# Scales of operands from norms summed by a matmul with ones, on one core, in place of maxima sent through small transfers

## The chip, the cores and the metric

The kernel runs on one core of one Trainium2 chip. A core has TensorE (PE; its weight loads are shown apart, as PEld), VectorE (DVE), ScalarE (ACT), GpSimd (POOL) and SyncE (SP, which here only issues transfers). Each of them works through its own instructions in the order in which they stand in the program, and waits on semaphores for the others. The metric is the device time of one execution in microseconds (us), the median of several.

## The reference

Three stages follow one another, in float32. The sizes are 2304 tokens and a width of 512.

```python
# 1. attention in chunks of 64 tokens, 8 heads of 64
scores = scale * np.matmul(q_c, k_c.transpose(0, 1, 2, 4, 3))
attn = np.exp(scores - np.max(scores, axis=-1, keepdims=True))
attn = attn / (np.sum(attn, axis=-1, keepdims=True) + 1e-09)
out = np.matmul(attn, v_c)
# 2. four experts, 512 -> 1024 -> 512
p = domain_probs / (domain_probs.sum(-1, keepdims=True) + 1e-09)
for e in range(E):
    out += p[:, e:e + 1] * (np.maximum(x @ w1[e], 0.0) @ w2[e])
# 3. a gated layer, 512 -> 1536 -> 512
g = x @ w_gate
return (g * (1.0 / (1.0 + np.exp(-g))) * (x @ w_val)) @ w_out
```

## The kernel before

Every matmul of stages 2 and 3 runs on float16 pairs: an operand is split into a high part (ACT) and a rest (mostly POOL, some DVE), and three float16 products replace one float32 product. float16 has little range, so each operand is first multiplied by a power of two that is worked out from its values: this is its **scale**, and how it is found is what the change is about.

Tokens go in three passes of 768, as six blocks of 128. Stage 2 has 16 **sets** of weights per pass (256 columns of `w1` each), stage 3 has 12. A set is seven half-size products in place of eight (Strassen's scheme, `PRODUCTS`), each 6 matmuls of 384 columns, into PSUM banks `x`, `z` and `w`; ACT copies intermediate sums (`p`, `u`) out of a bank before the next product adds to it, DVE adds them up (`sum_p`, `sum_u`), ACT and DVE make the float16 pair of the hidden layer (`hh`, `hl`). The second matmul of a layer (`y`, or `ox` and `oz`) is placed between the products. In pass 0 the weights come as float32 (`raw`), are scaled, summed, split and stored as float16 (`w`); passes 1 and 2 load the stored ones. The weights of stage 3 come as 64-bit floats and are converted by background tasks (`make_ops`) during passes 0 to 2.

The order is written by hand, as a program that is played out product by product. `now` counts products; `later(d, f)` calls `f` after product `now + d`. A background task advances once per product; `yield WAIT` in it is one product of delay. Attention of blocks 0 to 5 comes first, by a table of steps (`FIRST_BLOCKS`); blocks 6 to 17 (`rest`) are put in steps between the products of pass 0.

A scale before, for a set of `w1` that was loaded in pass 0: `greatest` (DVE) reduces 128x1024 values to one maximum per partition (`col`); `spread_out` writes this column to DRAM, `spread_in` reads it back as one row on all partitions (`row`), both on SP's queue; `spread_end` (DVE) reduces the row, `scale_of` makes the power of two, and ACT multiplies (`w1_scaled`). `w2` (`w2_scale_later`), the 64-bit sets (`spread`, `row`) and `wo` (`spread_wo`, `row_wo`) do the same. Only the first five scales go by `total`, a matmul of `ones` with a bfloat16 column, which leaves the sum over partitions on all of them. The attention output has a scale for each token (`att_scale`), from the maxima of the block's own `av` in PSUM.

Of the kernel before, what the change touches and what calls it, by code (L numbers as in the profile page):

```python
# [94 lines left out]
def attention_moe_gated(  # L95
# [26 lines left out]
    by_token = const.tile([P, NS], F32, name="by_token")  # L122
# [42 lines left out]
    def scale_of_norm(o, back, left, square, k):  # L165

        nc.vector.tensor_scalar_max(square, square, TINY)
        halve(o, square)
        flip(o, o)
        nc.vector.tensor_scalar(out=o, in0=o, scalar1=2.0 ** (k - 66), scalar2=None, op0=ALU.mult)  # L170
        flip(back, o)
        nc.vector.scalar_tensor_tensor(out=left, in0=square, scalar=o, in1=o, op0=ALU.mult, op1=ALU.mult)
# [16 lines left out]
    def total(col, name, where):  # L189
        pool, tag = where  # L190
        ps = pool.tile([P, 512], F32, tag=tag, name=f"total_{name}")[:, :1]
        nc.tensor.matmul(ps, ones, col, start=True, stop=True)
        return ps
# [200 lines left out]
    def att_sums(a):  # L394
        s = att[a]
        sm = st_p.tile([P, H], F32, tag="sm", name=f"sm{a}")
        part = s["hs"][:, :, :, : CH // 4] if a < HALF else pairs(s["e"])
        nc.vector.tensor_reduce(out=by_pair(sm), in_=part, op=ALU.add, axis=AX.X)
        nc.vector.tensor_scalar_add(sm, sm, EPS)
        s["rs"] = st_p.tile([P, H], F32, tag="rs", name=f"rs{a}")  # L400
        nc.vector.reciprocal(s["rs"], sm)

# [16 lines left out]
    def att_scale(a):  # L419
        s = att[a]  # L420
        ps = s.pop("av")
        tops = st_p.tile([P, H], F32, tag="tops", name=f"tops{a}")
        top = st_p.tile([P, 1], F32, tag="top", name=f"top{a}")
        own = by_token[:, a : a + 1]
# [8 lines left out]
        if a >= BLOCKS and a % BLOCKS == BLOCKS - 1:  # L433
            scaled_shares(a // BLOCKS)

    def scaled_shares(s):
        r = slice(s * BLOCKS, (s + 1) * BLOCKS)
        nc.vector.tensor_scalar(
            out=back[:, r].bitcast(I32), in0=by_token[:, r].bitcast(I32), scalar1=EXPONENT, scalar2=None, op0=ALU.bitwise_xor
        )  # L440
# [62 lines left out]
    def fetch_w1(n, own=True):  # L503
        r = raw1[n] = raw1_p.tile([P, 8, 2 * P], F32, tag="raw1", name=f"raw1_{n}")
        nc.sync.dma_start(r[:, 0:4], w1[weights_of(n)])
        if n >= NPAIRS:
            later(3, lambda: w1_scaled(n))
        elif own:
            col = small(f"col_{n}")
# [4 lines left out]
            def ended():  # L514
                o = small(f"sum_{n}")
                spread_end(f"w1_{n}", o, ALU.add)
                w1_scale_of(n, o)
                w1_scaled(n)

            later(8, ended)  # L520

    def w1_scale_of(n, bound):
        s, r = w1_scale[n], w1_back[n] = small(f"s1_{n}"), small(f"b1_{n}")
        scale_of(s, bound, 9)
        flip(r, s)
# [69 lines left out]
    def make_ops(sources, name, sums, stores, column, scaled):  # L595
# [16 lines left out]
        col = small(f"col_{name}")  # L612
        op = column(r, col)
        yield WAIT
        spread_out(name, col)
        yield WAIT
        yield WAIT
        spread_in(name)
        yield WAIT
        yield WAIT  # L620
        bound = small(f"bound_{name}")
        spread_end(name, bound, op)
        scale = small(f"scale_{name}")
        scaled(scale, bound)
# [10 lines left out]
    def make_set64(q, m):  # L635
        into = w_d[NPAIRS + 2 * q + m]
        stores = [(PRODUCTS[i][1], into[i]) for i in range(NPROD)]

        def column(r, col):
            rows = small(f"rows_{q}_{m}", 4)  # L640
            for half in range(2):
                nc.vector.tensor_reduce(
                    out=rows[:, 2 * half : 2 * half + 2],
                    in_=r[:, 2 * half : 2 * half + 2].rearrange("p b (k f) -> p k b f", k=2),
                    op=ALU.max, axis=AX.XY, apply_absolute_value=True,
                )
            nc.vector.tensor_tensor(out=rows, in0=rows, in1=rows, op=ALU.mult)
            nc.vector.tensor_reduce(out=col, in_=rows, op=ALU.add, axis=AX.X)
            return ALU.add

        def scaled(scale, bound):
            scale_of_norm(scale, again64[:, m, q : q + 1], left64[:, m, q : q + 1], bound, 12)

        return make_ops(
            (wg, wv)[m][q], f"{q}_{m}", lambda r, half: w_sums(r, nc.gpsimd, half), stores, column, scaled
        )

    def make_wo_ops(g, k):
# [10 lines left out]
        def column(r, col):  # L669
            greatest(col, r[:, 0:4].rearrange("p b f -> p (b f)"))  # L670
            return ALU.max

        def scaled(scale, bound):
            scale_of(scale, bound, 10)
            flip(again64[:, 2, 2 * g + k : 2 * g + k + 1], scale)
# [8 lines left out]
    def x1_norm(s, b, sum_):  # L684
        a = s * BLOCKS + b
        waste = t_p.tile([P, DM], F16, tag="waste", name=f"waste_{a}", bufs=1)
        nc.scalar.activation(waste, sum_, AF.Square, accum_out=norms[:, a : a + 1])

    def x1_bound(s):
# [5 lines left out]
        later(3, lambda: spread_in(f"x1_{s}"))  # L695

        def ended():
            spread_end(f"x1_{s}", bound, ALU.max)
            x1_left[p] = small(f"x1_left_{s}")
            scale_of_norm(x1_scale[p], x1_back[p], x1_left[p], bound, 10)  # L700
# [3 lines left out]
        later(5, ended)  # L704
# [70 lines left out]
    def w2_greatest(G, i):  # L775
        c = w2_cols[G, i] = small(f"col2_{G}_{i}")
        greatest(c, raw2[G, i].rearrange("p b f -> p (b f)"))

    def w2_col(G, dtype=F32):
        c0, c1 = w2_cols[G, 0], w2_cols[G, 1]  # L780
        o = small(f"cols2_{G}", 1, dtype)
        nc.vector.tensor_scalar(out=c1, in0=c1, scalar1=w1_back[2 * G + 1], scalar2=None, op0=ALU.mult)
        nc.vector.scalar_tensor_tensor(out=o, in0=c0, scalar=w1_back[2 * G], in1=c1, op0=ALU.mult, op1=ALU.max)
        return o

    def w2_scale_of(G, bound):
        s = small(f"s2_{G}")
        w2_back[G] = small(f"b2_{G}")
        scale_of(s, bound, 11)
# [9 lines left out]
    def w2_scale_later(G, d):  # L799
# [4 lines left out]
        def out():  # L804
            spread_out(f"w2_{G}", w2_col(G))

        def ended():
            o = small(f"sum2_{G}")
            spread_end(f"w2_{G}", o, ALU.add)
            w2_scale_of(G, o)  # L810
            w2_scaled(G, 0)
# [235 lines left out]
    def gather(G, b, y):  # L1047
# [5 lines left out]
        if part == 1:  # L1053
            if b == 0:
                pg[0] = sm_p.tile([P, BLOCKS], F32, tag="pg", name=f"pg_{G}")
                nc.vector.tensor_scalar(
                    out=pg[0], in0=shares_of[:, s * BLOCKS : (s + 1) * BLOCKS, g * NE // NG1], scalar1=w2_back[g], scalar2=0.125,
# [28 lines left out]
    with tc.manual_schedule():  # L1086
# [5 lines left out]
        sm_p = ctx.enter_context(tc.tile_pool(name="sm", bufs=3))  # L1092
        w_p = ctx.enter_context(tc.tile_pool(name="w", bufs=12))
# [86 lines left out]
        def own_col(n):  # L1180
            cols[n] = small(f"col_{n}", 1, BF16)
            greatest(cols[n], raw1[n][:, 0:4].rearrange("p b f -> p (b f)"))
# [18 lines left out]
        def at(stage):  # L1201
# [6 lines left out]
            "f": lambda n: fetch_w1(n, False), "F": fetch_w1, "k": att_load_v, "L": att_load,  # L1208
            "a": own_col, "b": own_scale, "A": lambda i: w2_greatest(0, i), "B": lambda i: own_col2(), "C": lambda place: own_scale2(place),
# [34 lines left out]
        for a in range(BLOCKS, NS + 2):  # L1244
            for stages in ((att_scores, a), (att_values, a - 2)), (), ((att_turn, a - 1),), ((att_out, a - 2),):
                these = [(stage, b) for stage, b in stages if BLOCKS <= b < NS]
# [3 lines left out]
        def next_of_rest():  # L1250
            for stage, a in rest.pop(0):
                stage(a, (psA, "a"))
# [60 lines left out]
        for j in range(4):  # L1313
            later(6 + j, lambda j=j: split_w2(1, j))
# [25 lines left out]
        for o in order:  # L1340
# [29 lines left out]
            if i == 0 and (n == FIRST or group_of(n) != group_of(n - 1)) and group_of(n) < NPASS * NG1:  # L1370
# [5 lines left out]
                elif n > FIRST:  # L1376
                    w2_scale_later(G, 4)
                    for j in range(4):
                        later(1 + j // 2, lambda G=G, j=j: fetch_w2(G, j))
                        later(10 + j, lambda G=G, j=j: split_w2(G, j))  # L1380
# [104 lines left out]
```

## Time and profile before

| what | value |
|---|---|
| median of 3 runs (lowest to highest) | 1409.56 us (1405.64 to 1409.64) |
| the profiled execution | 1412.3 us, of which 1410.2 us from the first to the last instruction |
| PE busy | 1206.8 us (86%) |
| DVE, ACT, POOL busy | 927.5 us (66%), 609.7 us (43%), 536.2 us (38%) |
| mean granted TensorE clock | 0.938 |

PE has the most work. Its idle time and its clock are what another order of the work can change; busy time of another engine counts only where PE comes to wait for it.

### The profile page before, as it was taken

The numbers are of one execution on the slowest core, as the hardware profiler recorded it, in microseconds if no ns is written. First come the engines' busy times: TensorE is split into PE (matmuls) and PEld (weight loads), VectorE is DVE, ScalarE is ACT, GpSimd is POOL, SyncE is SP. The second block draws the span as 40 slices with busy tenths as digits, with TensorE's granted clock in tenths as the row PEclk, the third lists the DMA queues.
The fourth block names the chain that finished last, engine by engine and source line by source line (L and its number), as shares of the span: only waits on it lengthen the run. The fifth ranks groups of instructions, "written<-read, shape, count | busy, mean of one in ns | idle before, by whom it ended". The sixth has DMA issues, their size and how long they took to land.

```text
span 1410.2 us, 21408 instructions
## 1 busy us (share of the span) xinstructions
PE 1206.8 (86%) x7221; PEld 703.4 (50%) x7221; DVE 927.5 (66%) x1852; ACT 609.7 (43%) x1285; POOL 536.2 (38%) x603
## 2 busy tenths in 40 slices
PE   6888858857476998887889987979999999999998
PEld 5554435423233554443445443435556667676666
DVE  7787566655575576556755565643766786687677
ACT  4534433433345544344445443432454354444442
POOL 5233222323466555555553465551013322222221
PEclk9998979878698999999999999999999999999999
DMA  7277637538565676756576577765447655454543
GB/s 219 82 130 203 143 125 170 106 129 225 96 161 155 188 190 197 188 131 192 148 232 170 138 171 198 199 155 178 127 127 196 202 181 180 137 186 149 185 130 109
DMA packets 191085, 230.08 MB, mean 163 GB/s; under 512 B 25584, under 2 KB 146544, under 8 KB 190976
## 3 DMA queue, kind: packets, MB, share of 16 engines
q1 hardware_dynamic: 190048, 227.25, 59.5%
q10 hardware_dynamic: 896, 1.44, 0.3%
q8 instruction: 56, 0.92, 0.3%
q14 instruction: 53, 0.43, 0.1%
q0 software_dynamic: 32, 0.04, 0.0%
HBM read 168.60 MB, written 60.05 MB: 162 GB/s over the span
## 4 chain that ended last, share of the span: by engine, by line
PE 39%; DMA 26%; DVE 17%; issue 7%; ACT 7%; POOL 3%; SPq 1%; DVEq 0%; POOLq 0%; ACTq 0%
PE lx L917 4%; PE lx L918 4%; PE lx L919 4%; PE oz L1035 4%; DMA row_w<-spread_w 3%; DMA spread_w<-col 3%; PE ox L1035 3%; DMA w<-w 3%; PE y L966 3%; PE y L970 3%; PE y L968 3%; DMA spread_wo<-col_wo 2%; PE lz L917 2%; DVE col L145 2%; PE lz L918 2%
## 5 line engine op out<-in xcount | busy, mean ns | idle before, releaser
L966 PE MATMUL y<-w,hh 128*128 128x512 f16 x576 | 224.9, 390 | 7.3 <-ACT hh L847 3.9
L970 PE MATMUL y<-w,hl 128*128 128x512 f16 x576 | 223.4, 388 | 7.8 <-DVE hl L848 7.8
L135 POOL TENSOR_TENSOR w<-raw,w 128x256 f16<-128x256 f32 (+1 forms) x156 | 127.2, 827 | 258.3 <-ACT w L134 205.7
L968 PE MATMUL y<-w,hh 128*128 128x512 f16 x576 | 223.6, 388 | 0.0
L918 PEld LDWEIGHTS <-w 128*128 128x128 f16 x1182 | 118.6, 100 | 167.4 <-issue 96.9
L135 POOL TENSOR_TENSOR ol<-sg,oh 128x384 f16<-128x384 f32 x72 | 75.3, 1054 | 316.5 <-ACT oh L134 260.2
L917 PEld LDWEIGHTS <-w 128*128 128x128 f16 x1182 | 118.4, 100 | 120.0 <-DMA w<-w 36.2
L919 PEld LDWEIGHTS <-w 128*128 128x128 f16 x1182 | 119.1, 101 | 83.8 <-issue 11.0
L847 ACT ACTIVATE hh<-sum_p 128x384 f16<-128x384 f32 x90 | 46.8, 520 | 156.8 <-DVE sum_p L905 156.8
L848 DVE SCALAR_TENSOR_TENSOR hl<-sum_p,hh 128x384 f16<-128x384 f32 x90 | 60.2, 669 | 72.8 <-ACT hh L847 72.8
L1064 DVE SCALAR_TENSOR_TENSOR acc<-y,pg,acc 128x512 f32<-128x512 f32 x126 | 90.6, 742 | 25.5 <-PE y L970 23.1
L970 PEld LDWEIGHTS <-hl 128*128 128x128 f16 x576 | 57.6, 100 | 82.5 <-DVE hl L848 11.5
L966 PEld LDWEIGHTS <-hh 128*128 128x128 f16 x576 | 57.8, 100 | 71.6 <-issue 8.0
L135 POOL TENSOR_TENSOR w_made<-raw,w_made 128x256 f16<-128x256 f32 x84 | 61.3, 738 | 81.3 <-ACT w_made L134 73.8
L968 PEld LDWEIGHTS <-hh 128*128 128x128 f16 x576 | 57.7, 100 | 66.9 <-issue 9.0
L917 PE MATMUL lz<-b22h,w 128*128 128x384 f16 x162 | 54.6, 337 | 33.7 <-ACT p L901 33.3
L917 PE MATMUL lx<-t2h,w 128*128 128x384 f16 x162 | 54.6, 337 | 32.4 <-ACT p L901 32.2
L905 DVE TENSOR_TENSOR sum_p<-lx,p 128x384 f32<-128x384 f32 x81 | 44.6, 551 | 42.2 <-PE lx L919 41.4
L134 ACT ACTIVATE w<-raw 128x256 f16<-128x256 f32 (+1 forms) x156 | 67.6, 450 | 0.7 <-DVE raw L539 0.3
L917 PE MATMUL lz<-t1h,w 128*128 128x384 f16 x162 | 56.5, 349 | 12.8 <-DMA w<-w 12.6
L917 PE MATMUL lx<-t3h,w 128*128 128x384 f16 x162 | 53.3, 329 | 13.2 <-ACT u L901 8.4
L917 PE MATMUL lx<-b11h,w 128*128 128x384 f16 x162 | 55.2, 341 | 9.3 <-DMA w<-w 9.3
(282 smaller groups left out, 3012.3 us busy)
## 6 DMA issues: line engine op xcount, KB each, us to landing
w<-w SPq DMA_DIRECT2D x567, 128.0 KB, 3.6
w<-w SPq DMA_DIRECT2D x96, 256.0 KB, 4.9
w<-w_made SPq DMA_DIRECT2D x84, 128.0 KB, 4.7
raw<-w SPq DMA_DIRECT2D x19, 512.0 KB, 5.2
wo_t<-wo_t SPq DMA_DIRECT2D x36, 256.0 KB, 3.3
raw<-w SPq DMA_DIRECT2D x32, 256.0 KB, 4.8
sums<-x SPq DMA_DIRECT2D x40, 192.0 KB, 4.6
xt<-sums SPq DMA_DIRECT2D x40, 192.0 KB, 3.4
```

Source lines behind the costliest of these rows:

```text
L134: nc.scalar.activation(h, src, AF.Copy)
L135: (lo or nc.vector).tensor_tensor(out=l, in0=src, in1=h, op=ALU.subtract)
L847: nc.scalar.activation(h, src, AF.Relu)
L848: nc.vector.scalar_tensor_tensor(out=l, in0=src, scalar=0.0, in1=h, op0=ALU.max, op1=ALU.subtract)
L917: nc.tensor.matmul(ps, w[:, 0, c], xh[:, k], start=f, stop=False, skip_group_check=True)
L918: nc.tensor.matmul(ps, w[:, 0, c], xl[:, k], start=False, stop=False, skip_group_check=True)
L919: nc.tensor.matmul(ps, w[:, 1, c], xh[:, k], start=False, stop=e, skip_group_check=True)
L966: nc.tensor.matmul(y, hh[:, c], w[:, 0], start=(j == 0), stop=False)
L968: nc.tensor.matmul(y, hh[:, c], w[:, 1], start=False, stop=False)
L970: nc.tensor.matmul(y, hl[:, c], w[:, 0], start=False, stop=(j == 3))
L1035: nc.tensor.matmul(o, left[:, c], w[:, k, right], start=start and t % 2 == 0 and k == 0 and i == 0, stop=k == 1 and i == 2, skip_group_che ...
L1064: nc.vector.scalar_tensor_tensor(out=sum_, in0=y, scalar=p, in1=sum_, op0=ALU.mult, op1=ALU.add)
```

## The change

Maxima become sums of squares. `squares` is one ACT instruction over 128x1024 values that writes its squares to a scratch tile and their sum per partition to a column; `total` sums the columns over partitions on PE, and `scale_by_norm` (two DVE instructions on the bits of a number) makes a power of two from it. So for `w1` and `w2`, DVE's `greatest` becomes ACT's `squares`; for those and for the 64-bit weights, `spread_out`, `spread_in` and `spread_end` become one `total`. For attention, the scale of a token from `av` becomes a scale of the block from the norm of its `v` (`att_norm`, `att_norms`), which goes into the sum of the exponentials (`att_sums`), and four small DVE instructions and a reduction of `av` leave `att_scale`. The scale of a pass of stage 3 (`x1_bound`) keeps its transfers, with later steps. Exponents of the scales and some distances in products are changed with it.

```diff
+    def squares(x, col, name):
+        waste = wa_p.tile([P, 8 * P], F16, tag="waste", name=f"waste_{name}")
+        with nc.allow_low_precision("a bound, which is rounded to a power of two"):
+            nc.scalar.activation(waste[:, : x.shape[1]], x, AF.Square, accum_out=col)
+
+    def scale_by_norm(o, square, k):
+
         halve(o, square)
...
+        b = o.bitcast(I32)
+        nc.vector.tensor_scalar(out=b, in0=b, scalar1=-1.0, scalar2=float((189 + k) << 23), op0=ALU.mult, op1=ALU.add)
...
-        nc.vector.tensor_scalar_add(sm, sm, EPS)
+        nc.vector.tensor_scalar(out=sm, in0=sm, scalar1=EPS, scalar2=back[:, a : a + 1], op0=ALU.add, op1=ALU.mult)
...
+    def att_norm(a):
+        v = att[a]["v"].rearrange("p h i c d -> p (h i c d)")
+        squares(v, v_cols[:, a : a + 1], f"v{a}")
+
+    def att_norms(a, b, where):
+        r = slice(a, b + 1)
+        s = st_p.tile([P, b + 1 - a], F32, tag="vs", name=f"vs{a}")
+        scale_by_norm(s, total(v_cols[:, r], f"v{a}", where, b + 1 - a), 10)
+        flip(back[:, r], s)
...
-        greatest(tops, ps)
-        nc.vector.scalar_tensor_tensor(out=tops, in0=tops, scalar=TINY, in1=s["rs"], op0=ALU.max, op1=ALU.mult)
-        nc.vector.tensor_reduce(out=top, in_=tops, op=ALU.max, axis=AX.X)
-        flip(own, top)
-        nc.vector.tensor_scalar(out=s["rs"], in0=s["rs"], scalar1=own, scalar2=None, op0=ALU.mult)
...
-            later(3, lambda: greatest(col, r[:, 0:4].rearrange("p b f -> p (b f)")))
-            later(4, lambda: spread_out(f"w1_{n}", col))
-            later(6, lambda: spread_in(f"w1_{n}"))
...
-            later(8, ended)
+            col = small(f"col_{n}", 1, BF16)
+            later(3, lambda: squares(r[:, 0:4].rearrange("p b f -> p (b f)"), col, f"w1_{n}"))
+            later(5, lambda: w1_scale_of(n, total(col, f"w1_{n}", (psA, "a"))))
+            later(6, lambda: w1_scaled(n))
...
-        spread_out(name, col)
+        col = small(f"col_{name}", 1, BF16)
+        column(r, col)
         yield WAIT
         yield WAIT
-        spread_in(name)
+        scale = small(f"scale_{name}")
+        scaled(scale, total(col, name, (psA, "a")))
         yield WAIT
...
-        later(3, lambda: spread_in(f"x1_{s}"))
+        later(9, lambda: spread_in(f"x1_{s}"))
...
-        later(5, ended)
+        later(17, ended)
...
-        later(d + 2, out)
-        later(d + 4, lambda: spread_in(f"w2_{G}"))
-        later(d + 6, ended)
-        later(d + 7, lambda: w2_scaled(G, 1))
+        col = []
+        later(d + 1, lambda: col.append(w2_col(G, BF16)))
+        later(d + 3, lambda: w2_scale_of(G, total(col[0], f"w2_{G}", (psA, "a"))))
+        later(d + 4, lambda: w2_scaled(G, 0))
+        later(d + 5, lambda: w2_scaled(G, 1))
```

Whole-program counts: `total` stands 5 times before and 58 times after; `squares` over 1024 values 0 and 50 times (18 blocks of `v`, 16 sets of `w1`, 16 tiles of `w2`); pairs of `spread_out` and `spread_in` 40 and 3 times.

**SP's queue**, in pass 0, around the scale of set 8 of `w1`. Before, the column of set 8 goes out, and the read of its row stands behind loads of two tiles of `w2`, of `q`, of the places `kbd` and of `vbd`:

```order
L178 DMA spread_w1_8_1947<-col_8_1829 128x1
L771 DMA w2_9_120<-w2_2_1_1840 128x1024
L549 DMA w_6_89<-w_6_5_1852 128x512
L771 DMA w2_10_121<-w2_2_2_1900 128x1024
L549 DMA w_6_89<-w_6_4_1906 128x512
L759 DMA raw2_3_0_1969<-w2 128x512 x2
L304 DMA q14_1984<-qt 128x512
L307 DMA kbd0_213<-kt 64x512 x2
L314 DMA vbd0_214<-vt 64x512 x2
L183 DMA row_w1_8_2043<-spread_w1_8_1947 128x128
```

The same place now:

```order
L764 DMA w2_10_121<-w2_2_2_1852 128x1024
L549 DMA w_6_89<-w_6_5_1856 128x512
L764 DMA w2_11_122<-w2_2_3_1904 128x1024
L549 DMA w_6_89<-w_6_4_1911 128x512
L752 DMA raw2_3_0_1979<-w2 128x512 x2
L313 DMA q14_1994<-qt 128x512
L316 DMA kbd0_216<-kt 64x512 x2
L323 DMA vbd0_217<-vt 64x512 x2
L549 DMA w_6_89<-w_6_6_1940 128x512
```

The two transfers of the scale are gone; the other transfers keep their order.

**DVE's queue** at the same scale. Before, the reduction of the row (`sum_8`) stands between the sums of attention block 11 and the sums of set 6 (`pg` and `acc` belong to the second layer):

```order
L401 RECIPROCAL rs11_2080<-sm11_2077 128x8
L187 TENSOR_REDUCE sum_8_2091<-row_w1_8_2043 128x1
L155 TENSOR_SCALAR s1_8_2093<-sum_8_2091 128x1
L148 TENSOR_SCALAR s1_8_2093<-s1_8_2093 128x1
L148 TENSOR_SCALAR b1_8_2094<-s1_8_2093 128x1
L145 TENSOR_REDUCE col2_3_0_2099<-raw2_3_0_1969 128x1
L1056 TENSOR_SCALAR pg_2_2126<-shares_of_66,b2_2_1813 128x6
L1064 SCALAR_TENSOR_TENSOR acc1_0_1045<-y_2_0_2113,pg_2_2126,acc1_0_1045 128x512
L905 TENSOR_TENSOR sum_p5_6_2142<-lx_6_1938,p5_6_2089 128x384
```

Now the scale of set 8 reads PSUM, some products earlier, and the scale of the `v` of block 11 stands ahead of its sums:

```order
L892 TENSOR_TENSOR sum_p1_6_1964<-lw_6_1957,p1_6_1950 128x384
L835 SCALAR_TENSOR_TENSOR hl_3_0_0_1967<-sum_p1_6_1964,hh_3_0_0_1966 128x384
L160 TENSOR_SCALAR s1_8_1972<-total_w1_8_1970 128x1
L174 TENSOR_SCALAR s1_8_1972<-s1_8_1972 128x1
L148 TENSOR_SCALAR b1_8_1973<-s1_8_1972 128x1
L356 TENSOR_REDUCE mx12_1998<-s12_1985 128x8
L364 TENSOR_TENSOR e12_2000<-s12_1985,mx12_1998 128x4x2x64
L443 TENSOR_TENSOR e10_1574<-av10_2003,rs10_1869 128x512
```

Nothing on DVE stands behind a transfer there any more, and both 128x1024 reductions of this place are off DVE.

**ACT's queue** at the same place, now. Before, this stretch had the same instructions without the two of line 168, and one split of a tile of `w2` that now stands earlier:

```order
L463 COPY xb9_1919<-xt9_1914 128x512
L168 ACTIVATE waste_v11_1922,v_cols_68<-vbd1_219 128x1024
L834 ACTIVATE hh_2_2_1_1932<-sum_u_5_1930 128x384
L168 ACTIVATE waste_w1_8_1938,col_8_1836<-raw1_8_1834 128x1024
L134 ACTIVATE w_6_6_1940<-raw1_6_1313 128x256
L888 COPY p1_6_1950<-lx_6_1943 128x384
L134 ACTIVATE w_6_7_1954<-raw1_6_1313 128x256
L834 ACTIVATE hh_3_0_0_1966<-sum_p1_6_1964 128x384
```

Two squares of 1024 values now stand ahead of the copy `p1` of set 6, which PE needs before its next product into bank `x`.

## Rows read from the trace of the kernel before

**Rows 1.** Busy time by stretch: us; PE, PEld, DVE, ACT, POOL; PE clock, DMA share, GB/s.
```profile
0.00:70.00 70.00, 52.64 (x419) 36.95 (x420) 52.23 (x129) 34.88 (x74) 28.15 (x49) 0.95 0.48 151
70.00:455.00 385.00, 273.91 (x1560) 148.12 (x1559) 246.34 (x516) 158.88 (x326) 142.85 (x161) 0.84 0.61 150
455.00:945.00 490.00, 427.93 (x2178) 217.95 (x2176) 301.66 (x577) 213.65 (x465) 257.11 (x285) 0.95 0.68 177
945.00:1410.20 465.20, 452.31 (x3069) 300.39 (x3067) 327.24 (x633) 202.30 (x423) 108.05 (x109) 1.00 0.53 162
```

**Rows 2.** Waits of DVE, whole span: total us, times, longest us.
```profile
DVE sum L187 <- DMA row_w<-spread_w: 78.1, 17, 11.6
...
DVE bound L187 <- DMA row<-spread: 33.0, 7, 9.5
...
DVE bound_wo L187 <- DMA row_wo<-spread_wo: 24.3, 5, 8.5
...
DVE x_bound L187 <- DMA row_x<-spread_x: 9.8, 3, 5.0
```

**Rows 3.** Transfers by name: count, KB each, median us to landing.
```profile
row_w<-spread_w SPq DMA_DIRECT2D x19, 64.0 KB, 4.2
...
spread_w<-col SPq DMA_DIRECT2D x12, 0.5 KB, 6.9
```

**Rows 4.** Timeline, 162 to 182 us: start, us, engine, instruction, idle before it.
```profile
162.33 0.32 SPq L178 DMA_DIRECT2D spread_w<-col  x1
...
171.21 2.29 SPq L307 DMA_DIRECT2D kbd<-kt  x2
...
175.14 0.58 SPq L183 DMA_DIRECT2D row_w<-spread_w  x1
...
178.81 0.28 DVE L187 TENSOR_REDUCE sum<-row_w 128x1 f32<-128x128 f32 x1 [7.70 <-DMA row_w<-spread_w]
...
179.56 1.15 ACT L529 ACTIVATE raw<-raw,s 128x1024 f32<-128x1024 f32 x1 [11.34 <-issue]
...
181.54 1.98 PE L409 MATMUL av<-vbd,et 128*64 128x128 f32 x16 [7.28 <-ACT xb L455]
```

**Rows 5.** Waits of TensorE, whole span.
```profile
PEld L917 <- DMA w<-w: 36.2, 16, 6.5
...
PE lz L917 <- ACT p L901: 33.3, 6, 15.4
```

**Rows 6.** Waits of SP's queue, whole span.
```profile
SPq L183 <- DMA spread<-col: 49.3, 9, 7.6
```

**Rows 7.** Busy time in one stretch without and one with waits for rows.
```profile
490.00:525.00 35.00, 35.00 (x193) 18.72 (x192) 23.91 (x47) 16.23 (x37) 17.45 (x19) 1.00 0.79 193
...
350.00:385.00 35.00, 15.11 (x53) 6.68 (x53) 18.00 (x37) 13.37 (x27) 13.75 (x14) 0.60 0.44 72
```

**Rows 8.** Groups of ACT by form: busy us, mean ns, idle before.
```profile
L529 ACT ACTIVATE raw<-raw,s 128x1024 f32<-128x1024 f32 x16 | 18.3, 1142 | 46.7 <-issue 46.4 <-DVE s L148 0.2
...
L687 ACT ACTIVATE waste<-acc 128x512 f16<-128x512 f32 x18 | 11.3, 630 | 27.3 <-DVE acc L1064 27.3
...
L687 ACT ACTIVATION_READ_ACCUMULATOR waste<-acc 128x1 f32 x18 | 3.4, 187 | 0.0
```

**Rows 9.** Groups of DVE by form.
```profile
L145 DVE TENSOR_REDUCE col<-raw 128x1 f32<-128x1024 f32 x28 | 33.7, 1211 | 0.0
...
L145 DVE TENSOR_REDUCE tops<-av 128x8 f32<-128x512 f32 x18 | 12.2, 679 | 2.2 <-PE av L409 2.1
...
L429 DVE TENSOR_SCALAR rs<-rs,by_token 128x8 f32<-128x8 f32 x18 | 5.2, 290 | 0.6
```

**Rows 10.** Timeline of PE around one matmul with ones.
```profile
48.05 0.17 PE L192 MATMUL total_w<-col,ones 128*128 128x1 bf16 x1
48.07 0.32 PE L917 MATMUL plz<-b11h,w 128*128 128x384 f16 x1
```

**Rows 11.** Waits of PE before the matmuls with ones, whole span.
```profile
PE total_w L192 <- DVE col L145: 5.5, 3, 3.7
```

More of the change, by code (lines that the diff above doesn't have):

```diff
@@ L121, in attention_moe_gated @@
     ones = const.tile([P, P], BF16, name="ones")
-    by_token = const.tile([P, NS], F32, name="by_token")
+    v_cols = const.tile([P, NS], BF16, name="v_cols")
     back = const.tile([P, NS], F32, name="back")
@@ L163, in halve, with scale_of_norm @@
         )
-    def scale_of_norm(o, back, left, square, k):
-        nc.vector.tensor_scalar_max(square, square, TINY)
-        halve(o, square)
-        flip(o, o)
-        nc.vector.tensor_scalar(out=o, in0=o, scalar1=2.0 ** (k - 66), scalar2=None, op0=ALU.mult)
+    def squares(x, col, name):
[3 more added lines that the diff above has]
+    def scale_by_norm(o, square, k):
+        halve(o, square)
+        b = o.bitcast(I32)
+        nc.vector.tensor_scalar(out=b, in0=b, scalar1=-1.0, scalar2=float((189 + k) << 23), op0=ALU.mult, op1=ALU.add)
+    def scale_of_norm(o, back, left, bound, square, k):
+        nc.vector.tensor_scalar_max(square, bound, TINY)
+        scale_by_norm(o, square, k)
         flip(back, o)
@@ L187, in spread_end, with total @@
         nc.vector.tensor_reduce(out=o, in_=spreads.pop(name), op=op, axis=AX.X)
-    def total(col, name, where):
+    def total(col, name, where, n=1):
         pool, tag = where
-        ps = pool.tile([P, 512], F32, tag=tag, name=f"total_{name}")[:, :1]
+        ps = pool.tile([P, 512], F32, tag=tag, name=f"total_{name}")[:, :n]
         nc.tensor.matmul(ps, ones, col, start=True, stop=True)
@@ L508, in fetch_w1 @@
         elif own:
-            col = small(f"col_{n}")
-            later(3, lambda: greatest(col, r[:, 0:4].rearrange("p b f -> p (b f)")))
-            later(4, lambda: spread_out(f"w1_{n}", col))
-            later(6, lambda: spread_in(f"w1_{n}"))
[L514 to L518, printed above, removed]
-            later(8, ended)
+            col = small(f"col_{n}", 1, BF16)
+            later(3, lambda: squares(r[:, 0:4].rearrange("p b f -> p (b f)"), col, f"w1_{n}"))
+            later(5, lambda: w1_scale_of(n, total(col, f"w1_{n}", (psA, "a"))))
+            later(6, lambda: w1_scaled(n))
     def w1_scale_of(n, bound):
         s, r = w1_scale[n], w1_back[n] = small(f"s1_{n}"), small(f"b1_{n}")
-        scale_of(s, bound, 9)
+        scale_by_norm(s, bound, 6)
         flip(r, s)
@@ L647, in column @@
             nc.vector.tensor_tensor(out=rows, in0=rows, in1=rows, op=ALU.mult)
-            nc.vector.tensor_reduce(out=col, in_=rows, op=ALU.add, axis=AX.X)
-            return ALU.add
+            nc.vector.tensor_reduce(out=rows[:, :1], in_=rows, op=ALU.add, axis=AX.X)
+            nc.vector.tensor_copy(col, rows[:, :1])
         def scaled(scale, bound):
-            scale_of_norm(scale, again64[:, m, q : q + 1], left64[:, m, q : q + 1], bound, 12)
+            square = small(f"square_{q}_{m}")
+            scale_of_norm(scale, again64[:, m, q : q + 1], left64[:, m, q : q + 1], bound, square, 12)
         return make_ops(
@@ L670, in column @@
             greatest(col, r[:, 0:4].rearrange("p b f -> p (b f)"))
-            return ALU.max
         def scaled(scale, bound):
-            scale_of(scale, bound, 10)
+            scale_of(scale, bound, 11)
             flip(again64[:, 2, 2 * g + k : 2 * g + k + 1], scale)
@@ L685, in x1_norm @@
         a = s * BLOCKS + b
-        waste = t_p.tile([P, DM], F16, tag="waste", name=f"waste_{a}", bufs=1)
-        nc.scalar.activation(waste, sum_, AF.Square, accum_out=norms[:, a : a + 1])
+        squares(sum_, norms[:, a : a + 1], f"x1_{a}")
     def x1_bound(s):
@@ L776, in w2_greatest @@
         c = w2_cols[G, i] = small(f"col2_{G}_{i}")
-        greatest(c, raw2[G, i].rearrange("p b f -> p (b f)"))
+        squares(raw2[G, i].rearrange("p b f -> p (b f)"), c, f"w2_{G}_{i}")
     def w2_col(G, dtype=F32):
@@ L788, in w2_scale_of @@
         w2_back[G] = small(f"b2_{G}")
-        scale_of(s, bound, 11)
+        scale_by_norm(s, bound, 13)
         flip(w2_back[G], s)
@@ L1092, in attention_moe_gated @@
         sm_p = ctx.enter_context(tc.tile_pool(name="sm", bufs=3))
+        wa_p = ctx.enter_context(tc.tile_pool(name="wa", bufs=2))
         w_p = ctx.enter_context(tc.tile_pool(name="w", bufs=12))
@@ L1181, in own_col @@
             cols[n] = small(f"col_{n}", 1, BF16)
-            greatest(cols[n], raw1[n][:, 0:4].rearrange("p b f -> p (b f)"))
+            squares(raw1[n][:, 0:4].rearrange("p b f -> p (b f)"), cols[n], f"w1_{n}")
         def own_scale(n, place):
@@ L1244, in attention_moe_gated @@
         for a in range(BLOCKS, NS + 2):
-            for stages in ((att_scores, a), (att_values, a - 2)), (), ((att_turn, a - 1),), ((att_out, a - 2),):
-                these = [(stage, b) for stage, b in stages if BLOCKS <= b < NS]
+            for stages in (
+                ((att_scores, a), (att_values, a - 2)), (), ((att_turn, a - 1),), ((att_out, a - 2), (att_norm, a)),
+            ):
+                these = [(stage, b) for stage, b in stages if (BLOCKS, BLOCKS + 2)[stage is att_norm] <= b < NS]
+                if not stages and BLOCKS + 2 < a < NS or a == NS and stages and stages[0][0] is att_scores:
+                    these.append((att_norms, a - 1))
                 if these or not stages and BLOCKS + 2 <= a < NS:
@@ L1251, in next_of_rest @@
             for stage, a in rest.pop(0):
-                stage(a, (psA, "a"))
+                if stage is att_norm:
+                    att_norm(a)
+                elif stage is att_norms:
+                    att_norms(a, a, (psA, "a"))
+                else:
+                    stage(a, (psA, "a"))
         tasks, running = [], []
@@ L1313, in attention_moe_gated @@
         for j in range(4):
-            later(6 + j, lambda j=j: split_w2(1, j))
+            later(4 + j, lambda j=j: split_w2(1, j))
         FIRST, LEAD = 3, 6
@@ L1379, in attention_moe_gated @@
                         later(1 + j // 2, lambda G=G, j=j: fetch_w2(G, j))
-                        later(10 + j, lambda G=G, j=j: split_w2(G, j))
+                        later(9 + j, lambda G=G, j=j: split_w2(G, j))
             if last_of_pass(n + 1) and i == 5:
```

36 lines of the change are left out of this document (9 added, 27 removed), and 6 rows, old and new, of the table FIRST_BLOCKS.

## The prediction

> **What bounds the kernel now.** I read the busy time by stretch first, to see where PE stands idle. Of its 1410.2 us span, PE is idle 17.4 us up to 70 us (first attention blocks), 111.1 us from 70 to 455 us (pass 0 with the rest of attention; 385.00 less 273.91), 62.1 us from 455 to 945 us (passes 1 and 2 with the conversion of the 64-bit weights), and 12.9 us after that [rows 1]. I call the two middle ones stretch A and stretch B. No other engine is full in either: in A, DVE is busy 64% and ACT 41%. So the idle time comes from the order in which things wait, and the waits say which.
>
> DVE's waits come next. It stands 78.1 us, in 17 pieces, before the reduction of a row that came back from DRAM (all in A), and 33.0, 24.3 and 9.8 us before the same reduction for the 64-bit sets, for `wo` and for the passes of stage 3 [rows 2]. The two transfers take a median of 6.9 and 4.2 us to land [rows 3]. That is not the whole wait. The timeline shows one: the column leaves at 162.33 us, but the read of the row is issued at 175.14 us, because SP's queue stood until 171.21 us before a load of `kbd` whose place was in use. DVE idles 7.70 us until 178.81 us; ACT, which waits for DVE's scale, idles 11.34 us; a copy to free a bank stands behind that on ACT; and PE idles 7.28 us [rows 4]. So DVE's wait reaches PE almost one for one, and in PE's list it carries another name: PE waits for a copy of ACT (33.3 us in 6 pieces for `p`). Later, mostly in B, it is a load of `w` that comes late (36.2 us) [rows 5], and SP itself stands 49.3 us before reading rows of 64-bit sets, with the loads of `w` behind it [rows 6].
>
> The clock goes with it. From 350 to 385 us PE is busy 15.11 of 35 us at a granted clock of 0.60; from 490 to 525 us it is busy all 35 us at 1.00, with DVE at 68% and ACT at 46% [rows 7]. Of the two levels, 1.2 and 2.4 GHz, a mean of 0.84 in A means 32% of 385 us, 123 us, at the lower one.
>
> **The change part by part.**
>
> *Transfers and rows removed.* 37 of 40 round trips go, and with them DVE's waits of 78.1 us in A and 57.3 us in B. What is late next? Stretches without such waits show how well this program flows: 2.8% idle after 945 us [rows 1]. For A, which also has attention on the same engines, I allow twice that, 6% or 23 us, so 111.1 - 23 = **88 us** come back. Bounds: 78 (DVE's waits, one for one) and 111 (all idle). In B, 2.8% of 490 is 14, so at most 48 us; some loads of `w` will still be late for other reasons, and I take **40 us**. The lowest that I can defend is 34, two thirds of PE's wait for `w` plus a few waits for `p`.
>
> *Clock.* In A, 123 us are at the lower level and at most 111 of them are idle, so 12 to 88 us (32% of 274 busy) of work run at half speed, and half of that comes back: 6 to 44 us, **25** as the middle. In B, 49 us are at the lower level; the gaps are short, so most of it is work, and 0 to 21 us come back; **12**.
>
> *Squares on ACT.* 50 new instructions over 1024 values. ACT over that size takes 1142 ns, and reading the accumulator 187 [rows 8], so 1.33 us each and 66 us in all; 36 of them, 48 us, lie in A. ACT is idle 226 us in A, but its work does not wait in a pool: two squares now stand ahead of the copy `p1` that PE needs one product later. So between 0 and 48 us reach PE; I take half, **24 us back**. On DVE 32 reductions of 1.21 us and, for 18 blocks, one of 0.68 us and four small ones of at most 0.29 us fall away [rows 9]; some 65 us, off the path once the waits are gone, so I count nothing for it (what it could give lies inside the 23 us of idle that I left in A).
>
> On this the Trainium skill speaks against the change: "ScalarE: Activation LUTs", Rules for kernel authors, says to multiply on VectorE rather than ScalarE, and What ACT_TABLE_LOAD costs, on the same page, gives about 186 ns + 0.833 ns per element, which makes an estimated 1.04 us for 1024 elements. By it the squares would cost 37 us in A where the rows make it 48, and half of that 19 in place of 24. The trace agrees with the rule as far as it goes: 1.33 us by rows is more than the 1.21 us that DVE needs.
>
> *Matmuls with ones.* 53 more. One that does not wait costs PE next to nothing: it starts at 48.05 us and the next matmul at 48.07 [rows 10]. Three of the five stood 5.5 us for a column, 3.7 at the longest [rows 11], but there the reduction ends just ahead of the matmul. Now `w1` has two products between square and matmul, the 64-bit sets two. So between 0.02 and 1.8 us each, 1 to 97 us; I take 0.2, near the lower end for that distance: **10 us back**. Their slots in PSUM are freed by a DVE instruction that stands directly behind.
>
> *The rest.* In the first 70 us, ACT gains 14 squares (19 us) and DVE, the busiest engine there with 52 of 70 us [rows 1], loses about as much; PE idles 17.4 us there, so within +-5 us, taken as 0. The later read of rows for stage 3 removes the last of the 9.8 us: **2 us**, at most 5. Stage 3's scales are needed a pass later, so a delay of 17 products is covered by that pass.
>
> *Sum.* 88 + 40 + 25 + 12 + 2 - 24 - 10 = 133 us. The profiled execution took 1412.3 us, so it would take 1279; it lies 2.7 us above the median of the runs shown, which makes **1277 us**.
>
> **The rivals.**
>
> *ACT becomes the bound of A.* With the squares, ACT has 159 + 48 = 207 us of work in A, and A would shrink to about 285 us: 73% busy in strict order, where the full stretch of [rows 7] had 46%. Then all 48 us reach PE and A's clock gives back only its 6: 88 + 40 + 6 + 12 + 2 - 48 - 10 = 90, **about 1320 us**. For it: PE already waits for copies of ACT. Against it: today ACT is mostly the one that waits for DVE.
>
> *The rows are not what holds.* When DVE no longer waits for a row, it may wait for ACT or POOL, whose splits run late as well, and the idle time only changes its name. Then the DVE and clock terms vanish and the matmuls remain: **about 1409 us**, within 0.3%, which is about what runs of this kernel can tell from no change. The timeline speaks against it, since ACT idled there for DVE's scale.
> "DMA: Bandwidth & Descriptors", Anatomy of one DMA, in the Trainium skill, gives a transfer that GpSimd issues about 2.0 us plus its bytes; if that held for SP's too, both would take an estimated 4.2 us, the program's distance would cover them, and this rival would be the likely one. The trace disagrees: 6.9 and 4.2 us, before any queueing [rows 3].
>
> *PE stands at the matmuls with ones.* PE takes its instructions in order, so a late column stops everything. Without their term the gain is 143 us; over 53 matmuls that is 2.7 us each, and from there on the change loses. At the longest wait seen, 3.7 us, they cost 196 us: 1412.3 - 143 + 196 - 2.7, **about 1463 us**. For it: the wait exists, and squares wait for their load to land on ACT. Against it: two products of distance; DVE never waited for those loads at the same step (idle 0.0 before `col` [rows 9]).
>
> **How the numbers follow.** The forecast, with its own range of 1230 to 1312, has 0.72; ACT as the bound, 1312 to 1360, 0.18; rows that don't matter, 0.05; PE at the matmuls, 0.05. The range 1230 to 1350 holds nearly all of the first and most of the second. Its low end is A's 111, B's 48, both clocks at 35 together and 14 us of squares. Faster: 0.72 + 0.18 and part of the third, 0.92; same 0.03; slower 0.05.
>
> **What would show it.** In the changed profile, DVE's waits for rows should be gone but for those of `x_bound`, near 0; PE idle from 70 us to the end of pass 0 under 60 us, and its granted clock above 0.92 there; mean clock of the run above 0.97. Squares should take 1.3 us. If ACT is the bound, PE's waits for `p` and `u` stay at 30 us or more while ACT is busy over 75% in A. If the matmuls are, PE's list is led by waits before `total`. I am wrong on B if PE still waits 30 us for loads of `w`.

## The result, and the profile after

The changed kernel takes 1314.96 us (median of 4 runs, 1314.19 to 1316.42) against 1409.6: a ratio of 0.9335, 95% interval 0.9315 to 0.9354, 95 us faster. The prediction was 1277 us, with a range of 1230 to 1350; the direction and the range held, and 38 us of the 133 that I had worked out did not come.

Busy time by stretch in the changed kernel follows, with the columns of [rows 1]. The bounds are those of the same work: both programs have 5274 weight loads for the products and for `y`, in the same order, and 81.2, 412.7 and 851.3 us are where those loads start that were the first after 70, 455 and 945 us before.

```profile
0.00:81.20 81.20, 58.58 (x428) 39.54 (x429) 43.38 (x123) 51.65 (x107) 29.19 (x50) 0.85 0.44 143
81.20:412.70 331.50, 271.72 (x1590) 146.29 (x1589) 208.22 (x434) 194.52 (x397) 144.60 (x165) 0.90 0.52 168
412.70:851.30 438.60, 413.41 (x2194) 215.69 (x2193) 307.27 (x558) 215.38 (x471) 267.18 (x293) 0.98 0.64 199
851.30:1314.30 463.00, 451.33 (x3068) 300.17 (x3066) 325.44 (x629) 198.67 (x412) 99.61 (x96) 1.00 0.52 158
```

The start lost 11.2 us (81.2 for 70). Stretch A went from 385.0 to 331.5, B from 490.0 to 438.6, and the end from 465.2 to 463.0. PE's idle time fell from 111.1 to 59.8 us in A and from 62.1 to 25.2 in B. No wait for a row of a weight is left. What PE waits for now is another list; here are its longest waits in the changed kernel (total us, times, longest us):

```profile
PE total_w L201 <- ACT waste_w L168: 31.4, 14, 3.1
PE total L201 <- DVE col L643: 15.8, 5, 5.0
PE total_wo L201 <- DVE col_wo L145: 10.0, 3, 7.1
PE total_w L201 <- DVE cols L778: 9.2, 4, 5.7
PE total_v L201 <- ACT waste_v L168: 4.8, 2, 4.4
PE lx L904 <- ACT p L888: 4.4, 1, 4.4
```

Five of the six are matmuls with ones. All waits before a `total` add up to 82.6 us in 35 pieces, of 119.3 us that PE is idle; before, it was 8.4 us of 203.4. The waits for the copies `p` and `u`, through which the rows' delay had reached PE [rows 5], went from 73.9 to 6.3 us, so those copies were mostly a name that the delay had. In B, PE's waits for a late load of `w` went too; the 36.2 us of [rows 5] became 2.2.

A timeline of the changed kernel around one such wait, in A (start, us, engine, instruction, idle before it):

```profile
206.12 0.55 DVE L892 TENSOR_TENSOR sum_u<-lz,u 128x384 f32<-128x384 f32 x1
...
206.71 0.52 ACT L834 ACTIVATE hh<-sum_u 128x384 f16<-128x384 f32 x1 [2.34 <-DVE sum_u L892]
...
207.13 1.04 ACT L168 ACTIVATE waste_w<-raw 128x1024 f16<-128x1024 f32 x1
...
208.08 0.19 ACT L168 ACTIVATION_READ_ACCUMULATOR waste_w<-raw 128x1 bf16 x1
...
208.32 0.16 PE L201 MATMUL total_w<-col,ones 128*128 128x1 bf16 x1 [3.05 <-ACT waste_w L168]
```

ACT idled 2.34 us before `hh`, which waited for a sum of DVE, and the square stands behind `hh`. So the column is late although ACT has time to spare, and PE, which has nothing to do with that sum, stands 3.05 us. Two products of distance did not cover this chain through DVE and ACT. For a 64-bit set, in another stretch of the timeline, it is POOL that is late, since it ends the conversion that DVE then reduces:

```profile
347.44 1.33 POOL L592 TENSOR_TENSOR raw<-top,neg 128x512 f32<-128x512 f32 x1
...
348.98 1.27 DVE L636 TENSOR_REDUCE rows<-raw 128x2 f32<-128x512 f32 x2
...
350.95 0.16 DVE L643 CAST col<-rows 128x1 bf16<-128x1 f32 x1
...
351.16 0.16 PE L201 MATMUL total<-col,ones 128*128 128x1 bf16 x1 [5.02 <-DVE col L643]
```

### The profile page after: what moved, and what is told of

It is laid out like the page before. It is cut to its first block, busy times and chain, and to the rows that moved or that the text cites. A ratio compares the mean times of both kernels' runs of the same rounds, so it can differ in the third digit from the quotient of the medians.

```text
span 1314.3 us, 21379 instructions
## 1 busy us (share of the span) xinstructions
PE 1195.0 (91%) x7274; PEld 701.7 (53%) x7274; DVE 884.3 (67%) x1743; ACT 660.2 (50%) x1385; POOL 540.6 (41%) x603
## 4 chain that ended last, share of the span: by engine, by line
PE 61%; DVE 17%; ACT 9%; DMA 4%; issue 4%; POOL 2%; SPq 2%; DVEq 0%; ACTq 0%; POOLq 0%
PE y L953 7%; PE y L955 7%; PE y L957 7%; PE lx L904 5%; PE lx L906 5%; PE lx L905 5%; PE ox L1022 4%; PE oz L1022 4%; PE lz L904 3%; PE lz L906 3%; PE lz L905 3%; DVE hl L835 3%; ACT hh L834 2%; DMA w<-w 2%; DVE raw L539 2%
## 5 line engine op out<-in xcount | busy, mean ns | idle before, releaser
L953 PE MATMUL y<-w,hh 128*128 128x512 f16 x576 | 230.3, 400 | 6.2 <-DVE acc L1051 3.5
L957 PE MATMUL y<-w,hl 128*128 128x512 f16 x576 | 227.8, 396 | 2.1 <-DVE hl L835 1.8
L955 PE MATMUL y<-w,hh 128*128 128x512 f16 x576 | 229.7, 399 | 0.0
L904 PEld LDWEIGHTS <-w 128*128 128x128 f16 x1182 | 116.3, 98 | 111.0 <-issue 34.1
L905 PEld LDWEIGHTS <-w 128*128 128x128 f16 x1182 | 116.3, 98 | 86.2 <-issue 12.9
L906 PEld LDWEIGHTS <-w 128*128 128x128 f16 x1182 | 116.5, 99 | 78.4 <-issue 3.0
L957 PEld LDWEIGHTS <-hl 128*128 128x128 f16 x576 | 58.8, 102 | 78.5 <-issue 13.7
L134 ACT ACTIVATE oh<-sg 128x384 f16<-128x384 f32 x72 | 36.2, 521 | 61.7 <-DVE sg L853 61.3
L134 ACT ACTIVATE o<-sg 128x384 f16<-128x384 f32 x54 | 26.7, 518 | 66.1 <-DVE sg L205 66.1
L888 ACT COPY u<-lx 128x384 f32<-128x384 f32 x81 | 38.3, 472 | 34.2 <-PE lx L906 33.8
```

What stands on the lines that cost most here:

```text
L134: nc.scalar.activation(h, src, AF.Copy)
L904: nc.tensor.matmul(ps, w[:, 0, c], xh[:, k], start=f, stop=False, skip_group_check=True)
L905: nc.tensor.matmul(ps, w[:, 0, c], xl[:, k], start=False, stop=False, skip_group_check=True)
L906: nc.tensor.matmul(ps, w[:, 1, c], xh[:, k], start=False, stop=e, skip_group_check=True)
L953: nc.tensor.matmul(y, hh[:, c], w[:, 0], start=(j == 0), stop=False)
L955: nc.tensor.matmul(y, hh[:, c], w[:, 1], start=False, stop=False)
```

## The experiments

The theory after this reading was that distance is what is missing: the columns come a few us late, and a matmul with ones that stands later in the program would not wait. The rival was that ACT has too much to do with the squares, so that a wait cured here comes back elsewhere. In each of the three groups of runs below, the kernel before took 1429 to 1430 us, not 1410, while the changed kernel, which was repeated in one of them (e5), kept its time. So ratios are compared among the experiments alone, and times of changed kernels among each other.

### e5: the changed kernel again

No edit.

> The changed kernel as it is, to stand beside the others: in the last group of runs the kernel before took 1429 us where it had taken 1410, so ratios from different groups may not be set against each other. If the changed kernel moves with it, its ratio is again 0.933; if only the kernel before is slower there, the ratio is near 0.92.

1316.02 us, ratio 0.9207 (0.9172 to 0.9242). Only the kernel before had moved.

### e1: matmuls with ones two products later

```diff
-            later(5, lambda: w1_scale_of(n, total(col, f"w1_{n}", (psA, "a"))))
-            later(6, lambda: w1_scaled(n))
+            later(7, lambda: w1_scale_of(n, total(col, f"w1_{n}", (psA, "a"))))
+            later(8, lambda: w1_scaled(n))
...
         column(r, col)
         yield WAIT
         yield WAIT
+        yield WAIT
+        yield WAIT
...
-        later(d + 3, lambda: w2_scale_of(G, total(col[0], f"w2_{G}", (psA, "a"))))
+        later(d + 5, lambda: w2_scale_of(G, total(col[0], f"w2_{G}", (psA, "a"))))
```

The scaling and the splits of `w2` behind it move by two as well.

> Every matmul with ones of w1, w2, the 64-bit sets and wo is placed two products later (w1: 7 after the load in place of 5; the others likewise), what follows it too; nothing else. Theory (PE, which takes its work in order, stands before these matmuls because the columns come 1 to 5 us late, and distance cures it): PE's waits before the matmuls with ones, 80 us in the changed kernel, fall below 30, and the time from 1315 to between 1250 and 1280 us. Rival (ACT has too much to do since it makes the squares, so a wait cured here comes back elsewhere): PE's waits for the copies p and u rise by as much as the others fall, and the time stays between 1300 and 1320 us.

1272.79 us, ratio 0.8913 (0.8888 to 0.8939), 43 us less than the changed kernel. Its waits:

```profile
PE lx L906 <- ACT p L890: 11.6, 5, 4.3
PE total_w L201 <- ACT waste_w L168: 6.8, 3, 3.7
```

All waits before a `total` fell from 82.6 to 24.8 us. The waits for `p` and `u` rose from 6.3 to 14.4, so some of the rival is in it, 8 of 58 us. ACT's work is the same (busy 660.2 us in the changed kernel, 659.9 here). The stretches of the same work are now 74.8, 313.6, 418.4 and 464.4 us; here are the second and the third:

```profile
74.80:388.40 313.60, 267.21 (x1592) 147.71 (x1591) 204.18 (x444) 194.59 (x396) 143.12 (x159) 0.91 0.54 175
388.40:806.80 418.40, 407.66 (x2193) 213.63 (x2192) 296.21 (x559) 213.23 (x465) 262.43 (x288) 1.00 0.67 207
```

B has 10.7 us of PE idle time left, at a full clock. Distance was the theory, and it holds. PE's idle time fell by 30 us (119.3 to 89.1) and its busy time by 13 (1195.0 to 1182.1), so 58 us of waits that went gave back 43 us, not 58.

### e6: one product nearer

```diff
-            later(5, lambda: w1_scale_of(n, total(col, f"w1_{n}", (psA, "a"))))
+            later(4, lambda: w1_scale_of(n, total(col, f"w1_{n}", (psA, "a"))))
...
         column(r, col)
         yield WAIT
-        yield WAIT
```

`w2` and the steps behind them move by one as well.

> The matmuls with ones stand one product nearer to their columns than in the changed kernel (w1: 4 products after the load, w2 and the 64-bit sets likewise one less). Theory (distance): PE's waits before them rise from 83 us to between 110 and 160, and the time from 1315 to between 1335 and 1390 us. Rival (the waits are ACT's load under another name): the time stays within 10 us of the changed kernel's.

1368.01 us, ratio 0.9562 (0.9526 to 0.9597): 52 us slower than the changed kernel, for one product.

```profile
PE total L201 <- DVE col L642: 46.1, 11, 7.1
PE total_w L201 <- ACT waste_w L168: 37.1, 14, 4.5
PE total_wo L201 <- DVE col_wo L145: 16.4, 6, 5.6
```

The three kernels make a row: waits before `total` of 128.9, 83.6 and 24.8 us at distances -1, 0 and +2, and times of 1368, 1316 and 1273 us.

### e2: maxima on DVE, summed by matmuls

```diff
-            later(3, lambda: squares(r[:, 0:4].rearrange("p b f -> p (b f)"), col, f"w1_{n}"))
+            later(3, lambda: greatest(col, r[:, 0:4].rearrange("p b f -> p (b f)")))
...
-        squares(raw2[G, i].rearrange("p b f -> p (b f)"), c, f"w2_{G}_{i}")
+        greatest(c, raw2[G, i].rearrange("p b f -> p (b f)"))
```

> The columns of w1 and w2 are again maxima, reduced by DVE, but are summed by the matmul with ones; 32 squares leave ACT, 43 us. Theory (distance): a column from DVE is as late as one from ACT, the waits before the matmuls with ones stay above 50 us, and the time is between 1300 and 1335 us. Rival (ACT's load): ACT is relieved of two thirds of what the change gave it, and the time falls to between 1265 and 1295 us.

1324.06 us, ratio 0.9272 (0.9241 to 0.9303), 8 us above the changed kernel. All waits before a `total` add up to 93.1 us. Relieving ACT did not help, with DVE taking its reductions back in the same step; the late column now has DVE's name:

```profile
PE total_w L201 <- DVE col L145: 21.9, 8, 4.2
PE total_w L201 <- DVE cols L776: 17.8, 5, 11.1
```

### e8: squares done twice

```diff
+            later(3, lambda: squares(r[:, 0:4].rearrange("p b f -> p (b f)"), small(f"twice_{n}", 1, BF16), f"twice_{n}"))
             later(3, lambda: squares(r[:, 0:4].rearrange("p b f -> p (b f)"), col, f"w1_{n}"))
```

The same is done for `w2` from its second group on, on top of e1.

> Matmuls with ones two products later, and 26 squares of w1 and w2 in pass 0 done twice, the first time into a column that nobody reads: 35 us more on ACT, nothing else. Theory (distance, ACT has room): at most 10 us over the 1273 us of the same kernel without it. Rival (ACT's load reaches PE one for one): 25 to 35 us over. My prediction had half, 17 us.

1296.16 us, ratio 0.9072 (0.9036 to 0.9109), 23 us over e1. ACT's busy time rose by 27.7 us, from 659.9 to 687.6. So here 0.84 us reached the end for each us on ACT: ACT does not have room at this place, and the rival was closer than the theory on this point. Of the 24 us between the two profiles 18 are idle time of PE (89.1 to 106.7 us) and 6 are busy time at a lower mean clock (0.970 to 0.960). The first square of a pair also makes the column of the second later: waits before a `total` rose from 24.8 to 29.7 us, those for `p` and `u` from 14.4 to 21.4. So the run does not part ACT's load from a later column. The longest of PE's waits has ACT's name again:

```profile
PE lx L909 <- ACT p L893: 16.5, 6, 5.5
```

### e3 and e7: attention undone

The scale of attention's output is again by token, `FIRST_BLOCKS` as before; e3 on the changed kernel, e7 on e1.

```diff
-        nc.vector.tensor_scalar(out=sm, in0=sm, scalar1=EPS, scalar2=back[:, a : a + 1], op0=ALU.add, op1=ALU.mult)
+        nc.vector.tensor_scalar_add(sm, sm, EPS)
...
+        greatest(tops, ps)
+        nc.vector.scalar_tensor_tensor(out=tops, in0=tops, scalar=TINY, in1=s["rs"], op0=ALU.max, op1=ALU.mult)
+        nc.vector.tensor_reduce(out=top, in_=tops, op=ALU.max, axis=AX.X)
```

> The scale of the attention output is again one per token from maxima on DVE; the weights keep squares and matmuls with ones. 18 squares (24 us) leave ACT, 18 reductions with four small instructions (27 us) come back to DVE, 16 matmuls with ones fall away. Theory: the attention part is worth little by itself, between 1300 and 1330 us, and the first 70 us of work take 5 to 10 us less than in the changed kernel. Rival (ACT's load): 1280 to 1300 us.

> Matmuls with ones two products later, as before, and the scale of the attention output again by token from maxima on DVE. If the attention part costs about 6 us in the first blocks and nothing after (by the places of the weight matmuls), 1264 to 1270 us, against 1273 with it. If it relieves DVE where DVE matters once PE no longer waits, 1275 to 1290 us.

e3: 1312.25 us, ratio 0.919 (0.9162 to 0.9218). e7: 1268.12 us, ratio 0.8873 (0.8844 to 0.8901). Each is 4 to 5 us below its partner with the attention part, with intervals that overlap e5's and e1's. In e3 the load that started at 57 us before starts at 55.2, in the changed kernel at 61.0: the 6 us are there in the first blocks, and the difference is still 6 us at the load of 455. So the places in the traces show what the times alone do not.

### e9: only the transfers replaced

e7 with the maxima of e2: no square of 1024 values is left, and DVE has all its reductions back.

> Only the transfers are replaced: attention's scale by token and the maxima of w1 and w2 on DVE as in the kernel before, no square of 1024 values anywhere; matmuls with ones two products later than in the changed kernel. 50 squares (62 us by the changed kernel's trace) leave ACT, some 65 us come back to DVE. If moving work from DVE to ACT had no worth, within 8 us of the 1268 us of the same kernel with squares of w1 and w2. If ACT's load costs 0.67 us for each us, as the doubled squares showed, and DVE's costs nothing, 1240 to 1255 us. If DVE is the tighter one, 1280 to 1300 us.

1265.19 us, ratio 0.8858 (0.8813 to 0.8904), not to be told from e7. At this distance, moving the work from DVE to ACT was worth nothing; at the distance of the changed kernel, e2 without these squares was the slower one by 8 us.

### e4: matmuls with ones for the 64-bit sets and `wo` alone

The kernel before, with the changed `make_ops`:

```diff
-        spread_out(name, col)
         yield WAIT
         yield WAIT
-        spread_in(name)
...
+        scaled(scale, total(col, name, (psA, "a")))
```

> The kernel before, with the matmul with ones only for the 64-bit sets and wo: 18 of the 37 round trips go, no square is added. By the places of the weight matmuls in the two traces, the passes 1 and 2 gave back 51 of the 96 us. If that stretch is independent of the rest, 1350 to 1370 us. If the gain there came from what pass 0 no longer hands on (late work), it is less, 1375 to 1400 us.

1377.43 us, ratio 0.9637 (0.9607 to 0.9668): 51 us less than the kernel before of its group, and in the second of the two ranges. In pass 0 DVE still waits for its rows; its stretches A and B follow:

```profile
DVE sum L196 <- DMA row_w<-spread_w: 88.6, 18, 12.7
```

```profile
70.80:465.70 394.90, 273.56 (x1563) 149.66 (x1562) 245.70 (x515) 160.13 (x330) 143.27 (x164) 0.85 0.60 146
465.70:908.80 443.10, 414.67 (x2194) 216.41 (x2193) 309.13 (x559) 216.18 (x472) 268.01 (x295) 0.97 0.64 198
```

The reason written down for that range, late work that pass 0 hands on, is not what the trace shows. A is not shorter here (394.9 us, 385.0 before), and yet B takes 443.1 us where it took 490.0, against 438.6 in the changed kernel. So the 18 round trips give 47 of B's 51 us by themselves. The time missed the first range because A took 10 us more than in the profile before, in a group whose kernel before was slower as well; no trace of that one is there to compare.

### e11: the rows of stage 3 as before

```diff
-        later(9, lambda: spread_in(f"x1_{s}"))
+        later(3, lambda: spread_in(f"x1_{s}"))
...
-        later(17, ended)
+        later(5, ended)
```

> Attention undone, matmuls with ones two products later, and the row of a pass of stage 3 read back after 3 and used after 5 products, as in the kernel before, in place of 9 and 17. I took the change for 2 us, 5 at the most: 1270 to 1273 us against 1268. DVE waits for the row 5 to 10 us in three pieces.

1265.61 us, ratio 0.8865 (0.883 to 0.89), below the 1270 to 1273 that I expected and not to be told from e7. DVE does wait for these rows again, and it costs nothing that can be measured:

```profile
DVE x_bound L197 <- DMA row_x<-spread_x: 11.0, 3, 5.7
```

## Why the prediction was right in its range, and 38 us off

The range held, but by luck: the forecast's own range ended at 1312 us, and the result lies just above it, in the part that I had given to the rival in which ACT becomes the bound. That rival is not what happened, as is shown below. Of the 38 us that are missing, about 12 are idle time and 25 the clock. The terms for idle time (88 + 40 + 2 - 24 - 10) made 96 us, and PE's idle time fell by 84.1 (203.4 to 119.3). The clock's terms made 37, and PE's busy time, where the clock shows, fell by 11.8 (1206.8 to 1195.0).

*That the rows held PE* was right. Without their waits the copies that PE stood for came in time, and e4 shows the half in B by itself. The median landings of 6.9 and 4.2 us rest on one of 12 columns and five of 19 rows, the only ones whose landing the trace tells, so they are small samples. In the place of the 88 + 40 us that I took for both stretches, the kernel with enough distance (e1) gained 71.4 us in A (385.0 to 313.6) and 71.6 in B (490.0 to 418.4), clock included, where I had 113 and 52 with the clock. The squares' cost is still in the 71.4; but A of e9, which has none of them, takes 310.2 us, a gain of 74.8. So B had more to give than my bound from its idle time and my middle for its clock, and A less. That e1's 1273 us lie 4 us from my 1277 is therefore no confirmation: errors in both directions cancel there.

*The matmuls with ones* were the step that failed: I gave each 0.2 us, 10 in all, with the reason that two products lie between column and matmul. PE stood 82.6 us before them, 1.4 on average, which is near the upper end (1.8) that I had from the waits in the first blocks [rows 11] and set aside. 17.3 us of them lie before 81.2 us, 49.5 in A and 15.8 in B. In time they cost 43 us at the least: so much came back in e1, which still has 24.8 us of them. The mechanism was written down as the rival in which PE stands there. In the two waits shown above, what decided the size was not the two products, but what stands ahead of the square on ACT, or of the reduction on DVE, and what those in turn wait for. e6 and e1 show the size by distance. The point from which this rival would have made the kernel slower, 2.7 us each, was not reached even one product nearer (128.9 us over all 58, 2.2 each).

*Squares on ACT* were 1.33 us by the nearest rows; here is what they took in the changed kernel (groups by form, busy us, mean ns, idle before); below it are two of them with the matmul that needs both (timeline):

```profile
L168 ACT ACTIVATE waste_w<-raw 128x1024 f16<-128x1024 f32 x32 | 33.5, 1048 | 5.8 <-DMA raw<-w 5.8
L168 ACT ACTIVATE waste_v<-vbd 128x1024 f16<-128x1024 f32 x18 | 19.0, 1057 | 1.1 <-DMA vbd<-vt 1.1
...
L168 ACT ACTIVATION_READ_ACCUMULATOR waste_w<-raw 128x1 f32 x16 | 3.1, 195 | 0.0
```

```profile
57.23 1.04 ACT L168 ACTIVATE waste_v<-vbd 128x1024 f16<-128x1024 f32 x1
58.17 0.19 ACT L168 ACTIVATION_READ_ACCUMULATOR waste_v<-vbd 128x1 bf16 x1
58.26 1.04 ACT L168 ACTIVATE waste_v<-vbd 128x1024 f16<-128x1024 f32 x1
...
59.45 0.16 PE L201 MATMUL total_v<-v_cols,ones 128*128 128x2 bf16 x1 [4.38 <-ACT waste_v L168]
```

The square takes 1048 ns and its read 195, but they must not be added as I did: the records overlap, and the second square starts 1.03 us after the first. The 26 squares more of e8 raised ACT's busy time by 27.7 us, 1.07 each. Between e7 and e9, the 32 squares make 32.3 us of busy time on ACT (641.8 to 609.5) and what replaces them 29.5 us on DVE (883.3 to 912.8), so the 1.33 and 1.21 us of the rows were both too high and the difference between the engines is small. The Trainium skill's "ScalarE: Activation LUTs", What ACT_TABLE_LOAD costs, gave an estimated 1.04 us for the instruction alone, and the trace agrees (1048 ns). What a us on ACT costs I had as a half; e8 shows 0.84, with DVE unchanged. But I had counted DVE's relief at nothing, and e7 and e9 take the same time with the work on either engine: my 24 us back had a counterpart that I left out. Whether the two costs cancel or neither counts at that distance is not shown; no run takes the squares off ACT without giving DVE its reductions back. The rule of the Trainium skill that the prediction named from the same page, Rules for kernel authors, is neither borne out nor refuted by e7 and e9, which differ in just this choice for `w1` and `w2`.

*The rival that ACT becomes the bound*, at 1320 us, is 5 us from the result, and yet it is not what happened: PE waits 6.3 us for `p` and `u`, not over 30, and e1 takes 43 us less with the same work on ACT. e2, which takes 32 squares off ACT and gives DVE its reductions back, is not faster. ACT's busy share decides nothing here: it is 59% of A (194.5 of 331.5 us), and by the rival's own prices A would take 385 - 88 - 6 + 48 = 339 us, with ACT busy 61% of it, not the 73% of 285 us that I wrote. A time that fits does not show a cause. The sum of the rival in which the rows do not hold was off too: with the 10 us of matmuls that it keeps and the 2 us from stage 3 it makes 1418 us, and with the squares more, where I wrote 1409.

*The clock* followed the idle time: its mean went from 0.938 to 0.960, and time at the lower level from 174 to 106 us. I had expected more than 0.97 for the run and 0.92 in A; A has 0.90. With e1, 75 us at the lower level remain, and PE's busy time is 24.7 us less than before, still under the 37 that I took.

*The start* was not a zero: 11.2 us, of which 4.8 remain in e1. The rest came back in e1, whose waits before a `total` in this stretch fell from 17.3 to 13.7 us. The remainder belongs to the attention part: in e7, without it, the load that ends the start comes at 69.0 us. The wait of 4.38 us at 59.45 us, shown above, is most of it; a matmul with ones for two blocks stands there behind two squares on ACT, and e1, which leaves the order of the first blocks as it is, has the same wait. *The rows of stage 3*: 2 us expected, none measurable.

## What to carry to other kernels

A round trip through memory that an engine waits for in order can show up under other names: follow the wait back through the engines before believing the list of the last one. Replacing it by a small matmul is free only if its input is ready when the matmul's turn comes; count the distance from what the producer itself waits for, not in products between the two lines, and try one distance less and two more. When work moves from one busy engine to another, price both sides: here the time was the same with the work on either. And when two records of one engine overlap, take the time from one start to the next, not their sum.

## What the hardware showed that I had not expected

The kernel before took 1405.6 to 1410.6 us beside the changed kernel, and 1421.6 to 1433.3 in all three groups of experiments, while the changed kernel took 1315 and, in the one group that has it, 1316. The runs do not say why. One hint is in e4, which keeps the round trips of pass 0: there DVE waits 88.6 us for its rows, where it waited 78.1, and A takes 10 us more. It is one profile of another kernel, and does not show that the round trips are the cause. A distance of four products (e10) gave no result, and squares on POOL were not run.
